# Reordering the opening of a fused attention, Fourier-mix and MLP kernel: sine tables before the exps, casts moved to VectorE, first weights triggered sooner

## The chip, the cores and the metric

The kernel runs on one core of one Trainium2 chip. The metric is the device time of one execution in microseconds (us). Before the change it is 305.07 us, the median of three runs (304.42 to 305.32); the profiled execution has a span of 303.2 us.

Five engines work side by side [...]: TensorE (PE, matrix products), VectorE (DVE), ScalarE (ACT), GpSimd (POOL) and SyncE (SP, which issues most DMAs). Each engine executes its own instructions strictly in the order of the program.

## The reference

For each of 8 batches, 8 heads, 512 rows and 32 state rows with head width 64, two attentions without projections are computed and laid one below the other; then a Fourier mix over both axes and a two-layer MLP follow.

```python
scores = scale * x @ state^T;   xread = softmax(scores) @ state       # 512 rows a head
scores2 = scale * state @ x^T;  sread = softmax(scores2) @ x          # 32 rows a head
x = concat([xread, sread])      # reshaped to (8, 544, 512): heads beside one another
u = x + real(fft(fft(x, axis=1), axis=2))
un = (u - mean(u)) / sqrt(var(u) + 1e-6)
out = u + relu(un @ w_ch1) @ w_ch2        # 512 -> 2048 -> 512
```

The Fourier mix is done as matrix products with tables of cosines and sines, which the kernel makes itself at its start. `w_ch1` and `w_ch2` are 4 MB of float32 each; they are cast to bfloat16 on their way into the core's memory, which only GpSimd's DMA queue does here.

## The kernel before

The program goes through the batches as a pipeline: while the two layers of the MLP of batch b run, attention and transform of the next batches are woven in between. What the change touches is the opening, some 20 us in which batch 0 goes through attention and transform with nothing to overlap with.

The order of the instructions is fixed by hand. The loads of x: a batch is seven DMAs of 256-byte rows, 1 MB in all. Those of batch 0 are issued first; those of batch 1 follow on the SP queue.

```python
    def load_x(b):
        ...
        parts = [(v[:, 0], xb[1:129]), (v[:, 1], xb[144:272]), (v[:, 2], xb[273:401]), (v[32:128, 3], xb[416:512]),
                 (v[0:15, 3], xb[129:144]), (v[16:31, 3], xb[401:416]), (row, xb[0:273:272])]
        ...                                  # batch 0: spread over the SP and ACT queues
        for o, rows in parts:
            nc.sync.dma_start(out=o, in_=rows)

    def cast_x(b, copy=nc.gpsimd.tensor_copy, lo=0, hi=4):     # float32 xs -> bfloat16 xin, by tiles of 128 rows
        copy(xin_bufs[b % 2][:, lo:hi, 1:513], xs_of[b].rearrange("p (i c) -> p i c", i=4)[:, lo:hi])
```

ScalarE begins with a table load for the exp and casts tiles 2 and 0 of x:

```python
    nc.scalar.activation(gate2[:, 1:2], gate2[:, 0:1], AF.Exp)
    state_ones(0, 2)
    state_blocks(0, 1)
    cast_x(0, nc.scalar.copy, 2, 3)
    cast_x(0, nc.scalar.copy, 0, 1)
```

GpSimd's part: it clears pads, makes the integers of the second table, clears XB and ZB, casts tiles 3 and 1, sets constants, and then triggers the first three of the four blocks of `w_ch1`:

```python
    load_x(1)
    ...
    for lo, k0, c, t in (...):
        nc.gpsimd.tensor_scalar(gi[:, lo:lo + 128], ...)       # four of these
    nc.gpsimd.memset(XB..., 0.0)
    nc.gpsimd.memset(ZB..., 0.0)
    for i in (3, 1):
        cast_x(0, lo=i, hi=i + 1)
    constants()
    clears(0)
    def first_weights(lo, hi):
        for q in range(lo, hi):
            nc.gpsimd.dma_start(out=w1[:, :, q * 512:(q + 1) * 512], in_=w1v[:, :, q * 512:(q + 1) * 512])
    first_weights(0, 3)
```

The opening itself (read and score are batch 0's attention by tiles; low_of, terms_of and out_of its first transform; warm(n) is n small matmuls with no use but to keep TensorE busy):

```python
    warm(11); turn_state(); second_table(); warm(5)
    copy = turn_x0(2); copy(); turn_products(); warm(3)
    exp2 = score(2); exp2()
    copy = turn_x0(0); copy(); warm(2)
    copy3 = turn_x0(3); turn_ends(); copy3(); read(2); warm(3)
    exp0 = score(0); copy1 = turn_x0(1); exp3 = score(3)
    exp0(); exp3(); copy1(); warm(2); read(0)
    exp1 = score(1); exp1(); read(3)
    ...                                   # XB and ZB filled by VectorE and GpSimd
    first_weights(3, 4)
    second_weights()                      # four blocks of w_ch2
    warm(6); read(1)
    sin_table(); sine_c(); sine_s()       # table load, cosines TC, sines TS
    warm(4); sread(); begin(); warm(6); low_of(0, 1); state_rows()
    ...                                   # low_of, even, odd, terms_of; minus(NC, TC), minus(NS, TS) on VectorE
    nc.gpsimd.tensor_copy(gate, XO0s[:, 0, 0:4])
    for i in range(4):
        cast_x(1, lo=i, hi=i + 1)         # batch 1 of x, GpSimd
    state_blocks(1, 2, nc.gpsimd.tensor_copy)
    ...                                   # the last terms_of and out_of
    s1, r1 = attend(1)
    exp_again()
    over_d(0); add_sums(0, 1); centre_sums(0, 1); over_d(1)
    turns1()                              # TensorE: 16 transposes of batch 1's x, all four tiles
    ...
    load_x(2)
    turned[2, 0](); turn_u(0, 1); ...; warm(4)
    L[0]()                                # first step of the MLP of batch 0
```

Of the kernel before, what the change touches and what calls it, by code (L numbers as in the profile page):

```python
# [30 lines left out]
def kernel(  # L31
# [17 lines left out]
    NM = 288  # L49
# [30 lines left out]
    for hh in range(4):  # L80
# [3 lines left out]
    nc.gpsimd.iota(ltq[:, :, 64:128], pattern=[[-1, 2], [-2, 64]], base=271, channel_multiplier=0)  # L84
    nc.gpsimd.iota(ltq[:, :, 128:144].rearrange("p q (a i) -> p q a i", a=2), pattern=[[1, 2], [272, 2], [2, 8]],
                   base=129, channel_multiplier=0)
    nc.gpsimd.iota(li[:, 0:128], pattern=[[2, 128]], base=1, channel_multiplier=0)
    nc.gpsimd.iota(li[:, 128:256], pattern=[[2, 128]], base=2, channel_multiplier=0)
    make_identity(nc, ident)
    mirror = singles.tile([128, 128], BF16, name="mirror")  # L90
    halves = ((halfpi, PI / 2), (pi_pos, PI * (1.0 - 1e-6)), (epst, eps), (mhalf, -0.5))
    sg = singles.tile([128, 1], F32, name="sg")
# [2 lines left out]
    def constants():  # L95
        for t, v in halves:
            nc.gpsimd.memset(t, v)
# [49 lines left out]
    def cast_x(b, copy=nc.gpsimd.tensor_copy, lo=0, hi=4):  # L147
        copy(xin_bufs[b % 2][:, lo:hi, 1:513], xs_of[b].rearrange("p (i c) -> p i c", i=4)[:, lo:hi])  # L148
# [27 lines left out]
    gate = singles.tile([128, 4], F32, name="gate")  # L176
    gate2 = singles.tile([128, 4], F32, name="gate2")
    nc.vector.memset(gate2, 0.0)
    nc.scalar.activation(gate2[:, 1:2], gate2[:, 0:1], AF.Exp)
    state_ones(0, 2)  # L180
    state_blocks(0, 1)
    cast_x(0, nc.scalar.copy, 2, 3)
    cast_x(0, nc.scalar.copy, 0, 1)


    w1 = singles.tile([128, DC, dff], BF16, name="w1")
# [40 lines left out]
    def turn(W, N, lf, cols, scratch):  # L227
        n = len(cols)
        f2d, q2d = scratch[:, 0:n * W], scratch[:, n * W:2 * n * W]
        f, q = [t.rearrange("p (n w) -> p n w", w=W) for t in (f2d, q2d)]  # L230
        def ends():
            absolute(q2d, f2d)

        def products():
            for i, c in enumerate(cols):
                nc.vector.scalar_tensor_tensor(f[:, i, :], in0=lf, scalar=pf[:, c:c + 1], in1=q[:, i, :], op0=ALU.mult, op1=ALU.add)

        for i, c in enumerate(cols):
            nc.vector.tensor_scalar(q[:, i, :], in0=lf, scalar1=pn[:, c:c + 1], scalar2=float(1 << 23), op0=ALU.mult, op1=ALU.add)
        nc.vector.tensor_scalar(q2d, in0=q2d, scalar1=float(1 << 23), scalar2=-float(N), op0=ALU.subtract, op1=ALU.mult)  # L240
        return f, q, products, ends

    shrink = 1.0 - 1e-6
    nc.vector.memset(lt[:, 279:280], 0)
    nc.vector.memset(lt[:, 287:288], 272)
    nc.vector.tensor_copy(pf, pi_)
    lo_, up_ = pf[:, 2:3], pf[:, 1:2]
    nc.vector.tensor_scalar(up_, in0=lo_, scalar1=145.0, scalar2=None, op0=ALU.is_ge)
    nc.vector.scalar_tensor_tensor(lo_, in0=up_, scalar=-16.0, in1=lo_, op0=ALU.mult, op1=ALU.add)
    nc.vector.scalar_tensor_tensor(lo_, in0=lo_, scalar=144.0, in1=lo_, op0=ALU.is_lt, op1=ALU.mult)  # L250
    nc.vector.scalar_tensor_tensor(lo_, in0=up_, scalar=272.0, in1=lo_, op0=ALU.mult, op1=ALU.add)
    pn = singles.tile([128, 3], F32, name="pn")
    nc.vector.tensor_scalar(pn, in0=pf[:, 0:3], scalar1=1.0 / Stot, scalar2=None, op0=ALU.mult)
    f1, q1, turn_products, turn_ends = turn(NM, Stot, lt, [0, 2], gen1)
# [5 lines left out]
    def second_table():  # L260
        nc.vector.tensor_scalar(gi, in0=gi, scalar1=dm - 1, scalar2=None, op0=ALU.bitwise_and)
# [12 lines left out]
    def sin_table():  # L274
        nc.scalar.activation(gate2[:, 2:3], gate2[:, 0:1], AF.Sin)
# [12 lines left out]
    def clear_pads(i):  # L288
        nc.gpsimd.memset(XFs[i][:, :, 512:514], 0.0)
        nc.gpsimd.memset(XRs[i][:, :, 0:514:513], 0.0)  # L290

    def clears(i):
        if i == 0:
            nc.gpsimd.memset(XO[:, :, 0:257:256], 0.0)
            nc.gpsimd.memset(XOl[:, 0:257:256], 0.0)
        nc.gpsimd.memset(XNs[i].rearrange("p a b -> p (a b)"), 0.0)
        nc.gpsimd.memset(XQls[i].rearrange("p a b -> p (a b)").bitcast(F32), 0.0)

    nc.gpsimd.memset(xs_of[1][0:1, 0:1], 0.0)  # L301
    clear_pads(0)
    clear_pads(1)
    load_state(1, 2)
# [6 lines left out]
    nc.gpsimd.memset(XB.rearrange("p a c -> p (a c)").bitcast(F32), 0.0)  # L311
    nc.gpsimd.memset(ZB.rearrange("p n c -> p (n c)").bitcast(F32), 0.0)
    for i in (3, 1):
        cast_x(0, lo=i, hi=i + 1)
    constants()
    clears(0)
    def first_weights(lo, hi):
        for q in range(lo, hi):
            nc.gpsimd.dma_start(out=w1[:, :, q * 512:(q + 1) * 512], in_=w1v[:, :, q * 512:(q + 1) * 512])
# [250 lines left out]
    def open_batch():  # L570
# [15 lines left out]
            nc.vector.tensor_copy(sT, p[:, 0:512].rearrange("p (a b) -> p a b", b=128))  # L586

        def turn(si):
            p = ps0.tile([128, 1024], BF16, name="xTp", tag="t", bufs=2)
            for pr in range(4):  # L590
                nc.tensor.transpose(p[:, pr * 128:(pr + 1) * 128], xin[:, si, 1 + 128 * pr:129 + 128 * pr], ident)
            return lambda: (nc.vector.tensor_copy if si else nc.scalar.copy)(
                xT[:, :, 128 * si:128 * si + 128], p[:, 0:512].rearrange("p (a b) -> p a b", b=128))

        def score(si):
            p = es[si] = ps0.tile([128, 512], F32, name="esp", tag="t" if si == 1 else "e", bufs=2)
            lo = 128 * si
            pieces = {1: [(0, slice(lo + 127, lo - 1, -1))],
                      3: [(0, slice(lo, lo + 32)), (32, slice(lo + 127, lo + 31, -1))]}.get(si, [(0, slice(lo, lo + 128))])
            for g in range(2):  # L600
                for o, rows in pieces:
                    n = abs(rows.stop - rows.start)
                    for hp in range(2):
                        nc.tensor.matmul(p[:, 128 * g + o:128 * g + o + n], lhsT=sT[:, 2 * g + hp, :],
                                         rhs=xT[:, 2 * g + hp, rows], start=(hp == 0), stop=(hp == 1))
            for pr in range(4):
                hp, o = pr % 2, 256 + 64 * pr
                nc.tensor.matmul(p[:, o:o + 64].rearrange("p (h j) -> p h j", j=Ns), lhsT=xT[:, pr, lo:lo + 128],
                                 rhs=sT[:, pr, 64 * hp:64 * hp + 64].rearrange("p (h j) -> p h j", j=Ns)[:, :, ::-1],
                                 start=True, stop=True)  # L610
            return lambda: nc.scalar.activation(EE[:, si, :], p, AF.Exp, scale=scale)
# [80 lines left out]
    def transform(b):  # L692
# [9 lines left out]

        acc = {}

        def begin():
            for j, tag in enumerate("ttee"):
                acc[j] = ps0.tile([128, 512], F32, name="gp", tag=tag, bufs=2)
            for j in range(4):
# [314 lines left out]
    exp2()  # L1023
    copy = turn_x0(0)
# [12 lines left out]
    copy1()  # L1037
    warm(2)
    read(0)
    exp1 = score(1)  # L1040
    exp1()
# [15 lines left out]
    begin()  # L1057
    warm(6)
    low_of(0, 1)
    state_rows()  # L1060
    low_of(1, 1), low_of(2, 1), low_of(3, 1)
    even(1)
    minus(NC, TC)
    terms_of(0, 1), terms_of(1, 1)
    odd(1)
    minus(NS, TS)
    second_sines()
    second_halves()
    sine_low()
    low_of(0, -1), low_of(1, -1)  # L1070
    terms_of(2, 1), terms_of(3, 1)
    even(0)
    low_of(2, -1), low_of(3, -1)
    terms_of(0, 0)
    out_of(0)
    terms_of(1, 0)
# [146 lines left out]
```

## Time and profile before

| stage, us from the start of the span | PE busy | DVE busy | ACT busy | POOL busy | DMA share of 16 engines |
|---|---|---|---|---|---|
| 0 to 6 | 2.54 | 4.15 | 3.18 | 4.96 | 0.83 |
| 6 to 12 | 5.04 | 5.12 | 2.56 | 4.51 | 1.05 |
| 12 to 18 | 6.00 | 5.43 | 5.28 | 4.40 | 1.19 |
| 18 to 24 | 5.44 | 3.42 | 4.98 | 5.49 | 1.24 |
| 24 to 28 | 4.00 | 3.79 | 3.32 | 0.11 | 1.21 |
| 28 to 34 | 5.24 | 5.05 | 3.58 | 5.45 | 1.22 |

Each row is one stretch of the span with the busy time of the engines in it. [...] TensorE is busy nearly throughout from 6 us on, but in the opening much of that is warm-up matmuls, so its busy time there says nothing about need. The DMA engines are loaded from 2 us to about 38 us: first x, then the weights.

### The profile page before, as it was taken

To read this page: it belongs to the slowest core of one execution; us is meant where nothing else is said; L and a number is where in the kernel's file an instruction comes from. 1 tells how busy PE (TensorE), PEld (TensorE's weight loads), DVE (VectorE), ACT (ScalarE), POOL (GpSimd) and SP (SyncE) were. 2 spreads that over 40 slices of the span, in tenths; PEclk is the share of its full clock that TensorE was granted. 3 is DMA by queue.
4 is the path that set the end of the run, shared out by engine and by line. 5 is a ranking of instruction groups with operands and counts; after the bars stand their busy time and mean duration, and the time that the engine had idled before them with its cause. 6 is when DMAs were issued, how large, how long until landed. Compare 5 with 4: busy or idle time off the path is not lost.

```text
span 303.2 us, 6030 instructions
## 1 busy us (share of the span) xinstructions
PE 288.2 (95%) x2310; PEld 165.6 (55%) x2341; DVE 182.1 (60%) x447; ACT 133.2 (44%) x248; POOL 92.9 (31%) x220
## 2 busy tenths in 40 slices
PE   4999897889999999999999999999999999999996
PEld 3889885444544545456544554445444544555443
DVE  7878895677879385755727575675668474000012
ACT  5687564436633553244533545244524442334300
POOL 6794564290371044301315022702240031000000
PEclk9999999999999999999999999999999999999999
DMA  8999954944934954459332695253333123600345
GB/s 156 191 204 198 203 99 98 214 90 104 175 88 71 205 131 82 105 93 220 95 81 55 146 183 90 68 121 77 82 91 69 37 69 87 138 3 35 71 132 145
DMA packets 110794, 34.86 MB, mean 115 GB/s; under 512 B 101950, under 2 KB 106302, under 8 KB 110766
## 3 DMA queue, kind: packets, MB, share of 16 engines
q1 hardware_dynamic: 100046, 28.72, 45.2%
q0 software_dynamic: 4224, 4.19, 8.3%
q10 hardware_dynamic: 6496, 1.57, 2.5%
q8 instruction: 18, 0.29, 0.4%
q14 instruction: 10, 0.08, 0.1%
HBM read 22.41 MB, written 14.02 MB: 120 GB/s over the span
## 4 chain that ended last, share of the span: by engine, by line
PE 76%; SPq 9%; DVE 5%; POOL 5%; DMA 2%; issue 2%; ACT 0%; POOLq 0%; DVEq 0%
PE po L978 34%; PE ph L914 32%; SPq L145 7%; PE gp L777 2%; SPq L387 1%; PE po L970 1%; DMA gen<-s_dram 1%; POOL stb L168 1%; DMA xs<-in_x_dram 1%; PE yp L674 1%; POOL w L324 1%; PE yp L673 1%; PE esp L431 1%; PE eTp L443 1%; PE xfp L456 1%
## 5 line engine op out<-in xcount | busy, mean ns | idle before, releaser
L978 PE MATMUL po<-w,hT 128*128 128x512 bf16 x481 | 122.2, 379 | 1.3 <-issue 0.6
L916 ACT ACTIVATE hT<-ph 128x512 bf16<-128x512 f32 x112 | 66.8, 597 | 121.2 <-PE ph L914 115.4
L914 PE MATMUL ph<-unT,w 128*128 128x512 bf16 x432 | 112.0, 379 | 0.7
L914 PEld LDWEIGHTS <-w 128*128 128x128 bf16 x576 | 50.6, 98 | 46.6 <-issue 0.5
L978 PEld LDWEIGHTS <-hT 128*128 128x128 bf16 x496 | 46.7, 98 | 46.6
L945 DVE SCALAR_TENSOR_TENSOR ot<-po,rstd,U 128x512 f32<-128x512 f32 (+2 forms) x33 | 24.1, 731 | 51.2 <-PE po L978 49.0
L781 POOL COPY GL<-G 128x128 bf16<-128x128 bf16 x7 | 2.0, 291 | 73.1 <-ACT G L778 73.1
L678 DVE TENSOR_TENSOR U<-yp,XR 128x512 f32<-128x512 f32 x14 | 9.5, 681 | 24.6 <-PE yp L674 24.6
L342 POOL TENSOR_TENSOR rstd<-mv,epst 128x1 f32<-128x1 f32 x34 | 8.1, 238 | 45.6 <-DVE mv L338 45.6
L336 DVE BATCH_NORM_STATS2 st<-U 128x6 f32<-128x512 f32 x32 | 21.8, 682 | 0.0
L343 POOL TENSOR_TENSOR rstd<-rstd,mhalf 128x1 f32<-128x1 f32 x34 | 20.4, 601 | 2.7
L924 PE MATMUL ph<-unT,w 128*128 128x128 bf16 x256 | 15.8, 219 | 0.3 <-DVE unT L846 0.3
L778 ACT CAST G<-gp 128x288 bf16<-128x288 f32 x28 | 13.1, 481 | 6.6 <-PE gp L777 6.5
L924 PEld LDWEIGHTS <-w 128*128 128x128 bf16 x256 | 14.8, 98 | 0.6 <-issue 0.4
L148 POOL CAST xin<-xs 128x512 bf16<-128x512 f32 (+1 forms) x11 | 13.3, 1233 | 1.6 <-DMA xs<-in_x_dram 1.6
L836 DVE TENSOR_SCALAR ub<-U,mv 128x512 bf16<-128x512 f32 x24 | 12.2, 508 | 1.1 <-DVE mv L338 0.3
L926 ACT ACTIVATE hT<-ph 128x512 bf16<-128x512 f32 x16 | 9.5, 596 | 6.3 <-PE ph L924 6.3
L513 POOL COPY XT<-XR 32x514 bf16<-32x514 bf16 x6 | 3.6, 603 | 22.7 <-DVE XR L465 22.6
L465 DVE TENSOR_TENSOR XR<-xrp,rs 128x512 bf16<-128x512 f32 x14 | 9.7, 694 | 0.5
L465 DVE TENSOR_TENSOR XF<-xfp,rs 128x512 bf16<-128x512 f32 x14 | 9.7, 692 | 0.5
L1010 PE MATMUL warm<-ident 128*128 128x128 bf16 x54 | 6.2, 261 | 3.5 <-POOL xs L301 3.5
L678 DVE TENSOR_TENSOR U<-yp,XF 128x510 f32<-128x510 f32 x14 | 9.5, 676 | 0.0
(240 smaller groups left out, 376.3 us busy)
## 6 DMA issues: line engine op xcount, KB each, us to landing
xs<-in_x_dram SPq DMA_DIRECT2D x22, 256.0 KB, 4.2
w<-in_moe_w_ch_dram POOLq DMA_DIRECT2D x8, 512.0 KB, 11.6
out_dram<-ot SPq DMA_DIRECT2D x15, 256.0 KB, 3.5
r_dram<-ot SPq DMA_DIRECT2D x14, 256.0 KB, 2.3
out_dram<-r_dram SPq DMA_DIRECT2D x14, 256.0 KB, 3.6
xs<-in_x_dram SPq DMA_DIRECT2D x8, 192.0 KB, 4.6
xs<-in_x_dram ACTq DMA_DIRECT2D x2, 256.0 KB, 5.6
l_dram<-ot SPq DMA_DIRECT2D x2, 256.0 KB, 2.0
```

The lines of the kernel that those rows point to most:

```text
L145: nc.sync.dma_start(out=o, in_=rows)
L148: copy(xin_bufs[b % 2][:, lo:hi, 1:513], xs_of[b].rearrange("p (i c) -> p i c", i=4)[:, lo:hi])
L336: nc.vector.bn_stats(st6, u)
L343: nc.gpsimd.tensor_tensor(rstd, rstd, mhalf, op=ALU.pow)
L465: nc.vector.tensor_tensor(ov, in0=p[ps, :, 0:256].rearrange("p g (h d) -> p g h d", d=D), in1=rs[ps].unsqueeze(3).to_broadcast([n, 2, 4, D ...
L678: nc.vector.tensor_add(u.rearrange("p (k r) -> p k r", r=2), p.rearrange("p (r k) -> p k r", r=2)[:, 0:u.shape[1] // 2, :], x.rearrange("p ...
L778: nc.scalar.copy(G[:, j, :].rearrange("p (i q) -> p q i", q=2), p[:, 0:NM].rearrange("p (q i) -> p q i", q=2))
L914: nc.tensor.matmul(ph[:, o:o + n], lhsT=w1[:, c, f * 128:(f + 1) * 128], rhs=un_of[key][:, c, :], start=(c == 0), stop=(c == DC - 1))
L916: nc.scalar.activation(hT[:, per * i:per * i + per, :].rearrange("p a b -> p (a b)"), ph, AF.Relu, scale=-1.0 / 512 if key == 0 else -1.0 ...
L924: nc.tensor.matmul(ph[:, o:o + 128], lhsT=w1[:, c, f * 128:(f + 1) * 128], rhs=un_of[key][:, c, 128 * r:128 * r + 128], start=(c == 0), st ...
L945: nc.vector.scalar_tensor_tensor(ot[:, cols], in0=po_of[i][:, 0:cols.stop - cols.start], scalar=rstd, in1=u[:, cols], op0=ALU.mult, op1=AL ...
L978: nc.tensor.matmul(po_of[i], lhsT=h_of[key][:, f, i * 128:(i + 1) * 128], rhs=w2[:, f, :], start=(f == 0), stop=(f == FC - 1))
```

## The change

It reorders the opening. The stated aims are four: the angles and the sine and cosine tables are made ahead of all exps; the last tiles of x are cast by VectorE; the negated tables NC and NS are made by ScalarE; the first weights are triggered sooner. With this go the places of some warm-up matmuls, PSUM tags, the splitting of the angle computation into smaller steps, and the order of the terms of the first transform.

```diff
+    make_identity(nc, ident)
     nc.gpsimd.iota(li[:, 0:128], ...)
     nc.gpsimd.iota(li[:, 128:256], ...)
-    make_identity(nc, ident)
...
-    nc.scalar.activation(gate2[:, 1:2], gate2[:, 0:1], AF.Exp)
+    nc.scalar.activation(gate2[:, 1:2], gate2[:, 0:1], AF.Sin)
     cast_x(0, nc.scalar.copy, 2, 3)
-    cast_x(0, nc.scalar.copy, 0, 1)
...
     def minus(o, i):
-        nc.vector.tensor_scalar(o, in0=i, scalar1=-1.0, scalar2=None, op0=ALU.mult)
+        nc.scalar.mul(o, i, -1.0)
...                       (angles: the same steps, pn for the two columns apart, memsets of lt behind pf)
     nc.gpsimd.memset(xs_of[1][0:1, 0:1], 0.0)
+    constants()
     clear_pads(0)
...
                                 op0=ALU.mult, op1=ALU.add)
-    nc.gpsimd.memset(XB..., 0.0)
-    nc.gpsimd.memset(ZB..., 0.0)
-    for i in (3, 1):
-        cast_x(0, lo=i, hi=i + 1)
-    constants()
-    clears(0)
-    first_weights(0, 3)
+    first_weights(0, 2)
...
-            return lambda: (nc.vector.tensor_copy if si else nc.scalar.copy)(
+            return lambda: (nc.scalar.copy if si == 1 else nc.vector.tensor_copy)(
...
+    turn_products()
+    turn_ends()
+    sine_s()
+    sine_c()
+    exp_again()
     warm(11)
     turn_state()
-    second_table()
     warm(5)
     copy = turn_x0(2)
     copy()
-    turn_products()
+    second_table()
     warm(3)
     exp2 = score(2)
     exp2()
+    for i in (0, 3, 1):
+        cast_x(0, nc.vector.tensor_copy, i, i + 1)
+    nc.gpsimd.tensor_copy(gate, xin_bufs[0][:, 1, 1:5])
+    nc.gpsimd.memset(XB..., 0.0)
+    nc.gpsimd.memset(ZB..., 0.0)
+    clears(0)
+    first_weights(2, 4)
     copy = turn_x0(0)
     copy()
-    warm(2)
     copy3 = turn_x0(3)
-    turn_ends()
     copy3()
-    read(2)
-    warm(3)
-    exp0 = score(0)
     copy1 = turn_x0(1)
-    exp3 = score(3)
-    exp0()
-    exp3()
     copy1()
     warm(2)
+    exp0 = score(0)
+    exp0()
+    read(2)
+    exp3 = score(3)
+    exp3()
     read(0)
...
-    first_weights(3, 4)
     second_weights()
-    warm(6)
+    warm(4)
     read(1)
+    sread()
+    begin(0, 1, 2, 3)
+    minus(NC, TC)
+    minus(NS, TS)
     sin_table()
-    sine_c()
-    sine_s()
-    warm(4)
-    sread()
-    begin()
-    warm(6)
-    low_of(0, 1)
+    warm(2)
+    low_of(0, 1), low_of(1, 1)
     state_rows()
...                       (low_of with both signs, then terms_of; second_sines and sine_low earlier)
```

The line `gate` that is added makes GpSimd wait until VectorE has cast tile 1 of x before it clears XB and triggers the other two blocks of `w_ch1`. The loads of x and of the states, the casts of batch 1, and everything from batch 1 on stay as they were, at the same places in their engines' orders.

More of the change, by code (lines that the diff above doesn't have):

```diff
@@ L236, in products, with counts, rests @@
                 nc.vector.scalar_tensor_tensor(f[:, i, :], in0=lf, scalar=pf[:, c:c + 1], in1=q[:, i, :], op0=ALU.mult, op1=ALU.add)
-        for i, c in enumerate(cols):
+        def counts(i):
+            c = cols[i]
             nc.vector.tensor_scalar(q[:, i, :], in0=lf, scalar1=pn[:, c:c + 1], scalar2=float(1 << 23), op0=ALU.mult, op1=ALU.add)
-        nc.vector.tensor_scalar(q2d, in0=q2d, scalar1=float(1 << 23), scalar2=-float(N), op0=ALU.subtract, op1=ALU.mult)
-        return f, q, products, ends
+        def rests():
+            nc.vector.tensor_scalar(q2d, in0=q2d, scalar1=float(1 << 23), scalar2=-float(N), op0=ALU.subtract, op1=ALU.mult)
+        return f, q, products, ends, counts, rests
     shrink = 1.0 - 1e-6
+    pn = singles.tile([128, 3], F32, name="pn")
+    f1, q1, turn_products, turn_ends, turn_counts, turn_rests = turn(NM, Stot, lt, [0, 2], gen1)
+    lo_, up_ = pf[:, 2:3], pf[:, 1:2]
+    nc.vector.tensor_copy(pf, pi_)
+    nc.vector.tensor_scalar(up_, in0=lo_, scalar1=145.0, scalar2=None, op0=ALU.is_ge)
+    nc.vector.tensor_scalar(pn[:, 0:1], in0=pf[:, 0:1], scalar1=1.0 / Stot, scalar2=None, op0=ALU.mult)
+    nc.vector.scalar_tensor_tensor(lo_, in0=up_, scalar=-16.0, in1=lo_, op0=ALU.mult, op1=ALU.add)
     nc.vector.memset(lt[:, 279:280], 0)
     nc.vector.memset(lt[:, 287:288], 272)
[L246 to L249, printed above, removed]
     nc.vector.scalar_tensor_tensor(lo_, in0=lo_, scalar=144.0, in1=lo_, op0=ALU.is_lt, op1=ALU.mult)
+    turn_counts(0)
     nc.vector.scalar_tensor_tensor(lo_, in0=up_, scalar=272.0, in1=lo_, op0=ALU.mult, op1=ALU.add)
-    pn = singles.tile([128, 3], F32, name="pn")
-    nc.vector.tensor_scalar(pn, in0=pf[:, 0:3], scalar1=1.0 / Stot, scalar2=None, op0=ALU.mult)
-    f1, q1, turn_products, turn_ends = turn(NM, Stot, lt, [0, 2], gen1)
+    nc.vector.tensor_scalar(pn[:, 2:3], in0=pf[:, 2:3], scalar1=1.0 / Stot, scalar2=None, op0=ALU.mult)
+    turn_counts(1)
+    turn_rests()
     gi = gen2[:, 0:512].bitcast(I32)
@@ L297, in clears, with first_weights @@
         nc.gpsimd.memset(XQls[i].rearrange("p a b -> p (a b)").bitcast(F32), 0.0)
+    def first_weights(lo, hi):
+        for q in range(lo, hi):
+            nc.gpsimd.dma_start(out=w1[:, :, q * 512:(q + 1) * 512], in_=w1v[:, :, q * 512:(q + 1) * 512])
     nc.gpsimd.memset(xs_of[1][0:1, 0:1], 0.0)
+    constants()
     clear_pads(0)
@@ L310 @@
                                 op0=ALU.mult, op1=ALU.add)
-    nc.gpsimd.memset(XB.rearrange("p a c -> p (a c)").bitcast(F32), 0.0)
-    nc.gpsimd.memset(ZB.rearrange("p n c -> p (n c)").bitcast(F32), 0.0)
-    for i in (3, 1):
-        cast_x(0, lo=i, hi=i + 1)
-    constants()
-    clears(0)
-    def first_weights(lo, hi):
-        for q in range(lo, hi):
-            nc.gpsimd.dma_start(out=w1[:, :, q * 512:(q + 1) * 512], in_=w1v[:, :, q * 512:(q + 1) * 512])
-    first_weights(0, 3)
+    first_weights(0, 2)
     def second_weights():
@@ L588, in turn @@
         def turn(si):
-            p = ps0.tile([128, 1024], BF16, name="xTp", tag="t", bufs=2)
+            p = ps0.tile([128, 1024], BF16, name="xTp", tag="r" if si == 1 else "t", bufs=2)
             for pr in range(4):
                 nc.tensor.transpose(p[:, pr * 128:(pr + 1) * 128], xin[:, si, 1 + 128 * pr:129 + 128 * pr], ident)
-            return lambda: (nc.vector.tensor_copy if si else nc.scalar.copy)(
+            return lambda: (nc.scalar.copy if si == 1 else nc.vector.tensor_copy)(
                 xT[:, :, 128 * si:128 * si + 128], p[:, 0:512].rearrange("p (a b) -> p a b", b=128))
         def score(si):
-            p = es[si] = ps0.tile([128, 512], F32, name="esp", tag="t" if si == 1 else "e", bufs=2)
+            p = es[si] = ps0.tile([128, 512], F32, name="esp", tag="t" if si in (1, 3) else "e", bufs=2)
             lo = 128 * si
@@ L703, in transform, with begin @@
         acc = {}
[L705 to L708, printed above, removed]
+        def begin(*js):
+            for j in js:
+                acc[j] = ps0.tile([128, 512], F32, name="gp", tag="eett"[j], bufs=2)
+            for j in js:
                 nc.tensor.matmul(acc[j][:, 0:NM], lhsT=XN[:, 0, :], rhs=xin_bufs[0][:, 0, 0:NM], start=True, stop=False)
@@ L1023 @@
     exp2()
+    for i in (0, 3, 1):
+        cast_x(0, nc.vector.tensor_copy, i, i + 1)
+    nc.gpsimd.tensor_copy(gate, xin_bufs[0][:, 1, 1:5])
+    nc.gpsimd.memset(XB.rearrange("p a c -> p (a c)").bitcast(F32), 0.0)
+    nc.gpsimd.memset(ZB.rearrange("p n c -> p (n c)").bitcast(F32), 0.0)
+    clears(0)
+    first_weights(2, 4)
     copy = turn_x0(0)
     copy()
-    warm(2)
     copy3 = turn_x0(3)
-    turn_ends()
     copy3()
-    read(2)
-    warm(3)
-    exp0 = score(0)
     copy1 = turn_x0(1)
-    exp3 = score(3)
-    exp0()
-    exp3()
     copy1()
     warm(2)
+    exp0 = score(0)
[3 more added lines that the diff above has]
+    exp3()
     read(0)
@@ L1047 @@
     nc.gpsimd.memset(XB[0:32, 1, 257:258], 0.0)
-    first_weights(3, 4)
     second_weights()
-    warm(6)
+    warm(4)
     read(1)
+    sread()
+    begin(0, 1, 2, 3)
+    minus(NC, TC)
+    minus(NS, TS)
     sin_table()
-    sine_c()
-    sine_s()
-    warm(4)
-    sread()
-    begin()
-    warm(6)
-    low_of(0, 1)
+    warm(2)
+    low_of(0, 1), low_of(1, 1)
     state_rows()
-    low_of(1, 1), low_of(2, 1), low_of(3, 1)
+    low_of(2, 1), low_of(3, 1)
     even(1)
-    minus(NC, TC)
+    second_sines()
+    second_halves()
+    low_of(0, -1), low_of(1, -1), low_of(2, -1), low_of(3, -1)
+    sine_low()
     terms_of(0, 1), terms_of(1, 1)
     odd(1)
[L1066 to L1070, printed above, removed]
     terms_of(2, 1), terms_of(3, 1)
     even(0)
-    low_of(2, -1), low_of(3, -1)
     terms_of(0, 0)
```

## The prediction

> **What bounds the kernel now.** I read three things in this order: the chain of work that ended last, the busy times by stage, and the DMA queues by stage. The chain and the stages:
>
> ```profile
> PE 76%; SPq 9%; DVE 5%; POOL 5%; DMA 2%; issue 2%; ACT 0%; POOLq 0%; DVEq 0%
> ```
> ```profile
> 0.00:22.00 22.00, 17.31 (x225) 15.14 (x226) 16.80 (x66) 14.64 (x27) 17.75 (x62) 1.00 1.06 183
> 22.00:43.00 21.00, 19.78 (x373) 18.94 (x371) 17.85 (x48) 14.24 (x26) 10.88 (x26) 1.00 1.07 181
> 43.00:75.00 32.00, 27.88 (x232) 15.14 (x234) 22.57 (x60) 15.44 (x30) 15.32 (x32) 1.00 0.55 117
> 75.00:303.00 228.00, 223.19 (x1490) 116.41 (x1513) 124.91 (x275) 88.85 (x167) 48.94 (x102) 1.00 0.47 102
> ```
>
> The columns are window, length, busy us of PE, PE weight loads, DVE, ACT, POOL, granted clock, DMA share, GB/s. TensorE carries the chain, and from 22 us on it idles only 1.2 + 4.1 + 4.8 us. So a microsecond gained or lost when the opening hands over at about 22 us moves the end, less what waits between 43 and 75 us can absorb. The rest of the chain (SPq, DMA) lies before 75 us: it runs through the loads of x. Hence the third view, the DMA queues; q1 is the SP queue (x), q0 GpSimd's queue (weights). First 9 to 12 us, x of batch 1 alone; then 26 to 36 us, x of batch 2 beside the weights:
>
> ```profile
> q1 hardware_dynamic: 2824, 0.71, 122.8%
> ```
> ```profile
> q0 software_dynamic: 1566, 1.55, 91.5%
> q1 hardware_dynamic: 1565, 0.39, 30.0%
> ```
>
> The columns are packets, MB and share of 16 engines. Alone, x moves at 2824/3 = 941 packets per us. Beside weights each queue moves 157 per us, packet for packet: x falls to a sixth. The SP timeline shows the same in its issues, seven each for batch 1 (before the weights) and batch 2 (among them):
>
> ```profile
> 6.97 5.03 SPq L145 DMA_DIRECT2D xs<-in_x_dram  x7
> ...
> 21.64 18.07 SPq L145 DMA_DIRECT2D xs<-in_x_dram  x7
> ```
>
> [...] the 128x576 step of the angles took 1.31 us beside GpSimd's work. [...] 11 matmuls of 128 columns at the start are spaced about 107 ns, the 16 transposes at 21.9 us about 56 ns.
>
> **The change part by part: the opening itself.** The three lines of VectorE and ScalarE that matter before:
>
> ```profile
> 4.88 1.31 DVE L240 TENSOR_SCALAR gen<-gen 128x576 f32<-128x576 f32 x1
> ...
> 7.34 1.29 DVE L236 SCALAR_TENSOR_TENSOR gen<-gen,pf 128x288 f32<-128x288 int32 x2
> 8.67 0.95 DVE L224 TENSOR_SCALAR gen<-gen 128x576 int32<-128x576 int32 x1
> ```
> ```profile
> 8.32 0.60 ACT L611 ACTIVATE EE<-esp 128x512 bf16<-128x512 f32 x1 [0.78 <-PE esp L608]
> ```
>
> Angles: the chain on VectorE starts at 2.54 now, released by the later integers of GpSimd; reordered it can start near 2.05. The steps to the end of the 1.31 took 3.6 us; the split of pn adds some 0.2, so about 5.7 (estimate), less if GpSimd contends less. Then signs 0.3, products 0.9 to 1.3 and absolute values 0.4 to 0.95: angles done at about 7.3 instead of 9.6. The sines (0.67 and 0.76) then end near 8.3, the table load and the dummy exp (1.28 + 0.1) near 9.7. **The first exp starts at about 9.7 instead of 8.32.** In return the table load and two sines that now lie at 13.06 to 15.80 become two negations and a table load. VectorE gets three casts (about 0.4 each by the spacing of like 128x512 float32 to bfloat16 operations, 1.2 in all), GpSimd loses 1.6. Nineteen warm-ups (56 to 107 ns each, 1 to 2 us) go, but most of them fill waits.
>
> Following the new order from there (scores 0.6 to 0.8, exp 0.6, reciprocal and product 0.9 a tile on VectorE), exp0 starts near 11.3, exp3 near 12.2, exp1 near 13; read(3) leaves VectorE near 14.2, and GpSimd's XB is ready at about 15.2. Now it is ready at 15.17, and low_of begins at 15.28. From there TensorE works without a gap to 20.14, and the same terms take the same 4.8 us. ScalarE is a near tie: its sequence up to sine_low ended at 19.30 and should end near 19.5. **Sum for the opening: 0.0, give or take 0.6 us**; the shorter tail behind the exps pays for their later start.
>
> **The weights.** Now GpSimd triggers them at 10.06, and q0's first packets appear near 12.4:
>
> ```profile
> 10.06 2.45 POOL L319 DMA_DIRECT2D w<-in_moe_w_ch_dram  x3
> ...
> 19.01 2.27 POOL L148 CAST xin<-xs 128x512 bf16<-128x512 f32 x4
> ```
>
> That is 2.4 us from trigger to flow, just as x of batch 1 finishes (its packets run from 8.0 to 13). After the change two blocks come directly behind the four integer operations, which end near 5.3; so they flow from 7.7, a little before x of batch 1 starts at 8.0. Two blocks are 2/8 of q0's 4224 packets, 1056; at 158 per us they last to about 14.4. The other two blocks wait for VectorE's cast of tile 1 (about 9.7) and GpSimd's clears (1.6), are triggered near 11.4 and flow from 13.8: no gap. The second weights, triggered near 15.3, join before those end. So q0 is never empty until 7.7 + 4224/158 = 34.4.
>
> x of batch 1 is 512 rows of 8 pieces, 4096 packets. Some 200 pass before the weights are at full rate; the remaining 3900 at 157 per us take 24.8 us: **x of batch 1 has landed at about 33 us instead of 13.** Nothing moves in its consumers: GpSimd casts it (the 19.01 line, which has no wait now), and TensorE has its transposes ahead of the MLP of batch 0:
>
> ```profile
> 21.89 1.06 PE L403 MATMUL xTp<-ident,xin 128*128 128x128 bf16 x16
> ```
>
> They need all four tiles. Landing 33 to 34, cast 0.6: they start at about 34.5, and TensorE stands still for 12.6 us. [...] Loss at this point 14.3. What comes back: the waits from 50 to 57 us (0.5 for a transposed x of batch 2, 1.2 + 1.2 behind it). Batch 2's loads are issued later but meet an empty weight queue, 4096/941 = 4.4 us, so its data should be ready about 8 us later while TensorE is 14 later; some 3 us of waits vanish. **Net +11, minus what a gap between q0's blocks gives: each 0.1 us of empty q0 passes some 80 packets more of x, half a microsecond of its landing.** I take off 1: about +10, 315.
>
> **The rivals.**
>
> *Rival 1, nothing starves.* If the weights flow later than 2.4 us after the trigger, or leave gaps, x of batch 1 mostly gets through. For it: x has slack from 13 to 19, some 6 us, and the added gate shows that someone thought of contention with x. Against it: the gate guards batch 0 only, and the trigger time follows from GpSimd's order. Then the sum of the opening rules: 303.5 to 306.
>
> *Rival 2, the whole gains.* The weights' queue ends 3 us earlier (34.4 for about 37.6), x of batch 2 lands sooner, the waits at 50 to 57 shrink, and the opening gains 0.5: 301 to 304. For it: the hole in the DMA traffic at 7.5 to 8.0 is filled. Against it: as in the main line, since total traffic is the same and only its order changes.
>
> *Rival 3, later exps alone cost.* ScalarE becomes the bound of the opening, with a fourth table load: 306 to 308. The chain before has ACT at 0%, which speaks for room.
>
> **Range and chances.** I give the starvation three quarters, with 308 to 320 and its middle near 315; a gap in q0 or a partly hidden wait is what makes it smaller. The rivals share the rest, nearly all within 2%. An eighth of the starvation falls under 311.2, where 2% ends. So 315.0, range 304.3 to 319.5; faster 0.03, same 0.27, slower 0.70.
>
> **What would show it.** Right: q0's first packets near 7.7; q1 near 157 per us from 8.5 on and x of batch 1 landing at 28 to 34; POOL's four casts waiting on DMA; a PE wait of 7 to 13 us on the 16 transposes; first exp at 9.3 to 10.2; low_of near 15.3. Wrong: casts at 18 to 19 without a wait, or q1 at 900 packets per us beside q0, or GpSimd's trigger well after 5.3. The opening's sum would be wrong if low_of began before 14.7 or after 16.

## The result, and the profile after

The change makes the kernel slower: **321.49 us**, the median of four runs (321.30 to 321.81), against 305.19 (304.42 to 305.57). The ratio is 1.0538, with a 95% interval of 1.0515 to 1.0561. That is 16.3 us more; the profiled execution has a span of 320.0 us instead of 303.2. The prediction was 315.0, with a range up to 319.5: it had the direction and the place, but not the size.

The chain of waits and the busy time by stage of the changed kernel; the columns are those of before (window, length, busy us of PE, weight loads, DVE, ACT, POOL, granted clock, DMA share, GB/s; a DMA share over 1 needs no second queue, since x alone had 122.8% before):

```profile
PE 81%; SPq 6%; DMA 5%; DVE 5%; issue 1%; ACT 0%; POOL 0%; ACTq 0%; POOLq 0%; DVEq 0%
```
```profile
0.00:22.00 22.00, 15.59 (x209) 12.42 (x209) 16.55 (x70) 17.27 (x31) 14.48 (x55) 1.00 1.06 175
22.00:43.00 21.00, 5.10 (x59) 4.68 (x59) 2.26 (x7) 2.10 (x3) 6.28 (x18) 0.59 0.99 168
43.00:75.00 32.00, 27.47 (x412) 22.52 (x414) 24.80 (x71) 18.48 (x34) 14.35 (x33) 1.00 0.39 84
75.00:303.00 228.00, 225.69 (x1539) 117.79 (x1566) 132.78 (x297) 97.02 (x184) 56.02 (x115) 1.00 0.45 100
```

Nearly the whole loss lies in the second row. TensorE is busy for 5.10 us of 21 there, where it was busy for 19.78, and its granted clock is 0.59. VectorE and ScalarE do next to nothing either. Only the DMA engines are full, with a share of 0.99. The chain says which DMA: its DMA share went from 2% to 5%, and 12.08 us of that are one piece, the landing of x of batch 1 from 24.74 to 36.82.

The DMA queues of the changed kernel from 13 to 34 us (queue, packets, MB, share of 16 engines), and its seven loads of x of batch 1 on the SP timeline (start, duration, what):

```profile
q0 software_dynamic: 3284, 3.26, 91.5%
q1 hardware_dynamic: 3280, 0.82, 29.9%
```
```profile
6.74 19.50 SPq L145 DMA_DIRECT2D xs<-in_x_dram  x7
```

q0, the weights, and q1, x of batch 1, pass equal numbers of packets for 21 us, 156 per us each, where x alone had 941; such equal counts are called turns below. Issuing its seven loads now takes SP 19.50 us instead of 5.03, while its queue drains at a sixth of its pace. What follows is on the timelines of GpSimd and of TensorE; the brackets hold the idle time before an instruction and what ended it:

```profile
3.81 2.22 POOL L321 TENSOR_SCALAR gen<-gen,pf 128x128 int32<-128x128 int32 x4
5.97 1.72 POOL L310 DMA_DIRECT2D w<-in_moe_w_ch_dram  x2
...
17.25 0.62 POOL L148 CAST xin<-xs 128x512 bf16<-128x512 f32 x1
23.46 0.61 POOL L148 CAST xin<-xs 128x512 bf16<-128x512 f32 x1 [5.59 <-DMA xs<-in_x_dram]
30.05 0.61 POOL L148 CAST xin<-xs 128x512 bf16<-128x512 f32 x1 [5.97 <-DMA xs<-in_x_dram]
37.39 0.61 POOL L148 CAST xin<-xs 128x512 bf16<-128x512 f32 x1 [6.74 <-DMA xs<-in_x_dram]
```
```profile
24.13 0.29 PE L405 MATMUL xTp<-ident,xin 128*128 128x128 bf16 x1 [3.69 <-POOL xin L148]
38.06 1.68 PE L405 MATMUL xTp<-ident,xin 128*128 128x128 bf16 x14 [13.64 <-POOL xin L148]
```

Before, the four casts ran without a wait from 19.01 and the 16 transposes began at 21.89. Now each cast waits for its own tile. TensorE has its turn at the transposes at 20.22, does two of the sixteen, and stands still for 3.69 and 13.64 us. The MLP of batch 0, much of which could run by then (in experiment 6 twelve steps of it run from 22.27 to 33.81), comes behind the transposes in TensorE's program.

### The profile page after: what moved, and what is told of

Its sections match the earlier page's. It is cut to its first block, busy times and chain, and to the rows that moved or that the text cites. A ratio compares the mean times of both kernels' runs of the same rounds, so it can differ in the third digit from the quotient of the medians.

```text
span 320.0 us, 6004 instructions
## 1 busy us (share of the span) xinstructions
PE 287.9 (90%) x2295; PEld 164.6 (51%) x2326; DVE 180.4 (56%) x449; ACT 134.9 (42%) x251; POOL 91.1 (28%) x219
## 4 chain that ended last, share of the span: by engine, by line
PE 81%; SPq 6%; DMA 5%; DVE 5%; issue 1%; ACT 0%; POOL 0%; ACTq 0%; POOLq 0%; DVEq 0%
PE po L980 34%; PE ph L916 32%; SPq L145 6%; DMA xs<-in_x_dram 5%; PE ph L926 3%; PE gp L779 2%; DVE st L338 1%; PE po L972 1%; PE yp L676 1%; PE xfp L458 1%; PE yp L675 1%; PE xrp L458 1%; PE eTp L445 1%; PE esp L433 1%; DVE U L680 1%
## 5 line engine op out<-in xcount | busy, mean ns | idle before, releaser
L405 PE MATMUL xTp<-ident,xin 128*128 128x128 bf16 x16 | 2.2, 305 | 17.3 <-POOL xin L148 17.3
L148 POOL CAST xin<-xs 128x2048 bf16<-128x2048 f32 (+1 forms) x9 | 11.9, 1321 | 18.4 <-DMA xs<-in_x_dram 18.3
L848 DVE COPY unT<-tp 128x512 bf16<-128x512 bf16 x8 | 3.3, 413 | 20.2 <-PE tp L847 20.2
L405 PEld LDWEIGHTS <-xin 128*128 128x128 bf16 x16 | 1.6, 141 | 17.8 <-POOL xin L148 17.7
```

## The experiments

All compare with the kernel before on the same chip, whose medians beside the three groups were 305.31, 304.79 and 305.28.

**1. The new opening with the weights late.** All four blocks of `w_ch1` are triggered where the changed kernel triggers its last two; nothing else differs from it.

```diff
-    first_weights(0, 2)
...
-    first_weights(2, 4)
+    first_weights(0, 4)
```

> The changed kernel with one thing undone: no block of w_ch1 is triggered ahead of the gate; all four are triggered behind the clears, near 10.1 us, where the kernel before had them. Theory A (x of batch 1 starves behind the weights, and nothing else costs): x of batch 1 lands near 13 us, GpSimd's casts wait on no DMA, TensorE's 16 transposes start near 20.2 us instead of 38, and the time is 303.4 (a gain of 1.67 us at the hand-over kept) to 305 (given back at waits for x of batch 2). Rival B (the later order of exps, four table loads and ScalarE's negations cost something later on): over 306. Rival C (a large part of the 16 us lies elsewhere, for instance in the order of the MLP): over 310.

Measured: 305.35 (304.40 to 307.21), ratio 1.0002 (0.9980 to 1.0025). The trigger comes at 10.03. GpSimd's timeline of this kernel shows the four casts in one piece, with nothing in brackets:

```profile
17.53 2.27 POOL L148 CAST xin<-xs 128x512 bf16<-128x512 f32 x4
```

So the two early triggers are the whole loss of 16 us, and the three other aims together are worth nothing that shows. Yet the opening hands over sooner in this profile: the first matmul of the last transform step (`yp`) starts at 19.75 instead of 21.02 (by estimate 0.5 to 0.8 of this is TensorE's clock, as the last section tells). By like instructions the kernel is 1.27 us ahead of the one before until 32 us, 0.66 ahead from 37 to 65, and 0.31 behind from 66 on. The first step is a copy on VectorE that here lies beside a clear by GpSimd (29.69 to 30.89); this kernel first, then before:

```profile
29.86 1.17 DVE L514 COPY XT<-XR 32x514 bf16<-32x514 bf16 x1
```
```profile
31.14 0.28 DVE L513 COPY XT<-XR 32x514 bf16<-32x514 bf16 x1
```

The second step is among TensorE's waits of this kernel between 15 and 75 us (what waited, for what, us in total, times, longest):

```profile
PE xrp L457 <- DVE XF L466: 1.5, 1, 1.5
PE esp L432 <- DMA xT<-xin: 1.2, 1, 1.2
```

Both waits were 0.5 before. `esp` is for the transposed x of batch 2, whose DMA is issued at 43.58 here and at 43.37 before; its extra 0.7 costs nothing, because the wait behind it, for ScalarE's `E`, is 0.5 here and was 1.2. It is `xrp` that takes 1.0. It waits for VectorE, which waits for a copy by GpSimd, and GpSimd for a load of states; GpSimd's casts of these states in this kernel and before:

```profile
60.37 2.98 POOL L168 CAST stb<-gen 32x640 bf16<-32x640 f32 x4 [4.60 <-DMA gen<-s_dram]
```
```profile
60.07 2.98 POOL L168 CAST stb<-gen 32x640 bf16<-32x640 f32 x4 [3.64 <-DMA gen<-s_dram]
```

SP issues that load behind the transposed x of batch 2 and the seven loads of batch 3, so it keeps its time when TensorE comes sooner.

**2. The old opening with two early weights.** The kernel before, with two blocks triggered behind the four integer operations, at 5.10.

```diff
+    for q in range(2):
+        nc.gpsimd.dma_start(out=w1[:, :, q * 512:(q + 1) * 512], in_=...)
     nc.gpsimd.memset(XB..., 0.0)
...
-    first_weights(0, 3)
+    first_weights(2, 3)
```

> The kernel before with one thing added: two blocks of w_ch1 are triggered directly behind the four integer operations, near 5.2 us; all else stays. Theory A: weights flow from 7.4 to 7.7 us, x of batch 1 gets some 155 packets per us until about 35, the 16 transposes start at 36 to 38 us, time 319 to 322. Rival B (it takes the new order as well): under 312.

Measured: 315.97 (314.90 to 319.20), ratio 1.0336 (1.0305 to 1.0367). The starvation comes without the new opening, but is smaller than I expected. The DMA queues of this kernel from 13 to 15 us say why:

```profile
q1 hardware_dynamic: 1106, 0.28, 69.0%
q0 software_dynamic: 200, 0.19, 55.7%
```

The first two blocks are through before the third, triggered at 9.59, flows in full, so q0 runs nearly empty for about a microsecond. In these 2 us x gets 1106 packets instead of 312, some 800 more, and from 17 to 19 us it gets 795, again some 480 more. Together that is 8 us of sharing at 156 per us, and x starts only a good 1 us later here. But the transposes begin at 34.95 against 38.06, no more than 3.1 us sooner: from 28 to 34 us x passes 507 packets beside 1049 of the weights, so it no longer has a turn for each of theirs, and the last tile still comes late. Whether some of the 16 DMA engines were done with x by then and others not isn't on record. This profiled execution took 319.20, so its trace accounts for less than half of the gap between the median of 315.97 and the 321.49 of the change.

**3. The first two blocks just behind the added gate**, which waits for VectorE's casts of batch 0.

```diff
-    first_weights(0, 2)
...
     nc.gpsimd.tensor_copy(gate, xin_bufs[0][:, 1, 1:5])
+    first_weights(0, 2)
```

> The changed kernel with its first two blocks triggered behind the gate but ahead of the clears, near 8.8 us, so that they flow from about 10.9. Theory A puts a number on it: alone, x of batch 1 has passed some 2540 of 4096 packets by then (counted in the trace of the kernel before); the other 1560 at 155 per us take 10 us, landing near 21 to 22; the transposes start near 22.5 instead of 20.2 and the time is 305 to 307. If the weights' time of trigger did not matter but only its being ahead of the clears, 318 or more; if it did not matter at all, the same as with the trigger behind the clears.

Measured: 306.74 (305.72 to 307.67), ratio 1.0047 (1.0027 to 1.0067). Trigger at 8.73, and three casts run without a wait. The fourth line of the four on GpSimd's timeline of this kernel, and TensorE's wait that it causes:

```profile
22.61 0.61 POOL L148 CAST xin<-xs 128x512 bf16<-128x512 f32 x1 [2.89 <-DMA xs<-in_x_dram]
```
```profile
PE xTp L404 <- POOL xin L148: 1.9, 1, 1.9
```

From 5.97 to 8.73 the trigger moves by 2.8 us, and TensorE's wait goes from 17.3 us to 1.9. It grows so steeply because x alone passes 941 packets per us, and beside weights 156: a microsecond that x loses alone costs six beside them.

**4. One block early, the rest behind the clears**, so that q0 has a gap.

```diff
-    first_weights(0, 2)
+    first_weights(0, 1)
...
-    first_weights(2, 4)
+    first_weights(1, 4)
```

> The changed kernel with one block instead of two triggered early; the other three behind the clears. Theory A: the block flows from 8.1 to 11.5 us, the others from 12.2; x of batch 1 gets 0.7 us at full rate in between, has passed about 1000 packets by 12.2, and the other 3100 at 155 per us take 20 us: landing near 32 to 33, transposes near 34, time 315 to 318. If only the first megabyte in the way counted (a queue that is served in turn, block by block), half of the loss: 311 to 313.

Measured: 315.30 in one run; transposes at 31.40 after a wait of 9.83. In the gap, from 11 to 13 us, q0 passes 51 packets and x 1904, more than I had allowed for. That is the same sharing as in 2 and 3, seen from the side of a gap.

**5. The weights of the second layer behind the casts of batch 1.** They are what keeps q0 full from about 20 us on.

```diff
-    second_weights()
...                       (behind the casts of batch 1, ahead of state_blocks)
+    second_weights()
```

> The changed kernel with the four blocks of w_ch2 triggered behind GpSimd's casts of batch 1 instead of ahead of them. Theory A (packet for packet, no matter which weight): w_ch1's 2112 packets flow from 8 to about 22; by then x of batch 1 has passed some 2100 of 4096, the rest goes at 941 per us, landing near 25, transposes near 26 instead of 38, TensorE stalls 5 to 6 us; time 308.5 to 311. If what counts is that two blocks are first in the way, 318 to 322.

Measured: 313.42 (312.82 to 314.28), ratio 1.0293 (1.0261 to 1.0326). x landed at 25.8, near what I expected, and the transposes began at 26.62, but the time is 2.4 us above my highest figure. TensorE also waited 2.3 us for the state blocks, which my edit had put behind four triggers on GpSimd, and its matmuls came at half rate until about 33.9, by estimate from their spacing: 32 of the MLP took 2.67 us from 32.36, and 1.95 from 23.93 in the kernel before. Half the stream of weights did about half the damage (a ratio of 1.0293 against 1.0538); how the rest of the loss divides between these two is not settled.

**6. Batch 1's attention behind twelve steps of the MLP of batch 0**, to see whether TensorE's order alone makes the wait cost.

```diff
-    turns1()
...                       (its copies, scores and reads follow it)
+    turns1()             (behind twelve steps of the MLP)
```

> The changed kernel with attention of batch 1 (its transposes, scores and reads) moved in the program behind the first twelve steps of batch 0's MLP, so that TensorE has work while x of batch 1 crawls in. Theory A (the loss is the in-order wait of TensorE, not the late data in itself): no wait on the transposes over 3 us, but batch 1's attention now has little beside it; time 311 to 317. Rival: if the late data itself moves the end (through GpSimd, the load of batch 2 and what follows), 320 to 322 as before.

Measured: 316.02 in one run. TensorE's wait for the cast shrinks from 17.3 us to 4.2, and the time falls by only 5.5. Batch 1's attention now runs with nothing beside it and brings waits of its own: 1.6 for `eTp` and 1.0 for `xfp` that the changed kernel doesn't have. It also runs on a slower clock: granted are 5 tenths of full speed in both slices of the page from 39.3 to 55.0 us, and 1.00 from 43 to 54 us in the changed kernel. So the order is what turns the late landing into standstill, but undoing it moves the loss more than it removes it.

**7. Two of batch 1's tiles on ScalarE's queue**, the weights as early as in the change.

```diff
+        held = parts[1:3] if b == 1 else []
         for o, rows in parts:
-            nc.sync.dma_start(out=o, in_=rows)
+            (nc.sync; the two held by nc.scalar, behind exp_again() of the opening)
```

> The changed kernel with two of the four tiles of batch 1 issued by ScalarE's queue instead of SyncE's, behind the table load near 8.5 us; the weights stay early. Theory A in its sharper form ([...] two queues get two turns): x of batch 1 gets some 270 packets per us instead of 155, lands near 25, transposes near 26; ScalarE loses about 1 us to the two issues; time 309 to 313. Rival (both hardware queues share one turn, or bytes are shared, not packets): 319 to 322.

Measured: 305.25 (303.99 to 308.84), ratio 1.0013 (0.9993 to 1.0033). I had expected 309 to 313. The profiled execution took 308.84, so the reading rests on its packets and issue times. The DMA queues of this kernel from 12 to 18 us; q10 is ScalarE's:

```profile
q0 software_dynamic: 824, 0.81, 79.6%
q1 hardware_dynamic: 812, 0.20, 25.8%
q10 hardware_dynamic: 808, 0.21, 15.5%
```

Three queues take equal turns, 135 to 137 packets per us each, so x has two turns of three and gets 270 per us. The edit did a second thing: SP's loads of batch 1 began at 5.78 instead of 6.74, and some 1400 packets of x passed between 8 and 10 us, where the change passes 94. Both should help, and this run doesn't separate them. In this execution TensorE still waits 4.3 us at the transposes; how long it waits in one of the median's time isn't on record.

**8. Late weights, and two tiles of batch 2 on ScalarE's queue**: can the opening's 1.3 us be kept if batch 2 lands sooner?

```diff
+        held = parts[1:3] if b == 2 else []
...
-    first_weights(0, 2)
...
-    first_weights(2, 4)
+    first_weights(0, 4)
```

> The version with all weights triggered near 10 us (the opening of the changed kernel without the starvation), and two of the four tiles of batch 2 issued by ScalarE's queue. There the hand-over gained some 1.3 us but waits for the transposed x of batch 2 gave it back. If two queues get two turns, batch 2 lands nearer to 37 than to 41.8, its transposes start at 41 to 42.5 instead of 43.6 and the time is 303.8 to 305.0. If the two issues hold ScalarE up near 22 us, or the end of w_ch2 is what pins the transposes, 305 to 307.

Measured: 304.50 (304.10 to 305.98), ratio 0.9992 (0.9977 to 1.0006). From 28 to 36 us the three queues pass 1094 packets each, to the packet. But the transposed x of batch 2 is issued at 44.39, no sooner than before, and TensorE waits 2.0 us for it (in an execution of 305.98). A second turn takes bytes from the weights, and the engines hardly move more in all: 207 GB/s here, 197 in experiment 1 in the same 8 us.

**9. Experiments 3 and 7 together**: weights behind the gate, two tiles of batch 1 on ScalarE's queue.

```diff
+        held = parts[1:3] if b == 1 else []
...
-    first_weights(0, 2)
...
     nc.gpsimd.tensor_copy(gate, xin_bufs[0][:, 1, 1:5])
+    first_weights(0, 2)
```

> A version meant to beat both: the changed kernel with its first two blocks triggered behind the gate (near 8.7 us, flowing from 10.9), and two tiles of batch 1's x on ScalarE's queue. By 11 us some 2700 of 4096 packets have passed; the rest at two turns (270 packets per us) lands near 16 to 17, so no wait on the 16 transposes; TensorE's hand-over is that of the new order (about 0.4 to 1.3 us sooner than before), and the weights end 1 us sooner, near 37. If the transposed x of batch 2 moves up with them, 303.5 to 304.5; if the loads of batch 2 pin it as they did with all weights at 10 us, 304.5 to 305.5.

Measured: **304.53** (303.83 to 305.27, 22 runs) against 305.28, ratio 0.9972 (0.9957 to 0.9986). No wait is left on the transposes. From 8 to 12 us x passes some 3500 of its 4096 packets and the weights 11, so here x is nearly through before there is anything to share. This is the version that beats both kernels, the one before by 0.8 us. Where the 0.8 comes from isn't shown: the profiled execution took 305.07, and its lead of 0.56 us is gone behind `xrp`, which waits 1.1 us as in experiment 1.

**10. The same with batch 2 on two queues as well.**

```diff
-        held = parts[1:3] if b == 1 else []
+        held = parts[1:3] if b in (1, 2) else []
```

> As the version with the first blocks behind the gate and two queues for batch 1, and two queues for batch 2 as well. Two queues for batch 2 did not make its tiles land sooner with all weights at 10 us, since the loads then end together with the weights; so the same time as with one queue for batch 2, within 0.3 us: 303.5 to 305.3.

Measured: 305.25 (304.48 to 307.00), ratio 0.9998 (0.9980 to 1.0016): nothing gained, as 8 would have it, and the 0.8 of experiment 9 is gone, where I had expected to keep it.

**11. The kernel before with GpSimd's clears of XB and ZB behind its casts**, to measure what they cost VectorE's angles.

```diff
-    nc.gpsimd.memset(XB..., 0.0)
-    nc.gpsimd.memset(ZB..., 0.0)
     for i in (3, 1):
         cast_x(0, lo=i, hi=i + 1)
     constants()
+    nc.gpsimd.memset(XB..., 0.0)
+    nc.gpsimd.memset(ZB..., 0.0)
```

> The kernel before with one thing moved: GpSimd's clears of XB and ZB (they ran from 5.1 to 5.9 us, beside VectorE's 128x576 step of the angles) behind its two casts. If GpSimd's clears are what slowed that step, it takes 0.5 to 0.7 us instead of 1.31, and the chain of angles ends 0.6 sooner; if the step is slow by itself in the old order, it stays at 1.2 to 1.4. Time: within 1 us of the kernel before, since waits on the loads of batch 2 take back what the opening gains.

Measured: 305.28 in one run. The step that took 1.31 us before, on VectorE's timeline of this kernel:

```profile
4.87 0.59 DVE L240 TENSOR_SCALAR gen<-gen 128x576 f32<-128x576 f32 x1
```

The hand-over comes at 19.50 instead of 21.02, from the old order of the opening with two lines moved, though part of this too may be an earlier full clock: VectorE's first two reciprocals of batch 0, the second of which waits for TensorE, start 1.51 us apart here and 2.18 before. Again the time doesn't follow: TensorE waits 1.4 us at `esp` and 1.6 at `xrp`.

## Why the prediction was right in kind and short in size

**The main line held.** Triggers behind the integers, turn by turn with x, four casts that wait, a standing TensorE, a slow restart (a granted clock of 0.50 from 38 to 40 us, 1.00 from 41 on): each is in the trace, and experiment 1 shows that without the early triggers nothing of the loss is left. Rivals 1 and 2 fall with the result, and so does rival 3, since experiment 1 keeps the new exps at 305.35.

**The failed steps are terms of the sum.** The prediction went 12.6 (standstill) + 1.7 (a slow clock behind it, the author's estimate, which the trace before didn't show) − 3 (comes back) − 1 (a gap) = about +10. Measured as shifts of like instructions between the two profiles:

| term | predicted | measured | from |
|---|---|---|---|
| transposes begin later | 12.6 | 16.2 | 38.06 against 21.89 |
| slow clock | 1.7 | 1.0 | first MLP matmul 41.11 against 23.93 |
| VectorE's `ub` slowed | – | 0.9 | next step 43.81 against 25.71 |
| comes back | −3 | −1.3 | shift 18.1 there, 16.8 at the end |
| gap in q0 | −1 | in the first row, about −1 | 307 packets of x from 11 to 12 us, beside 146 |
| **sum** | **10.3** | **16.8** | spans 320.0 and 303.2 |

*"x of batch 1 has landed at about 33 us"*: it landed at 36.8 (the chain's DMA, 24.74 to 36.82). The prediction's own formula, with three inputs mended, gives most of this. I let x start at about 8.2, but its first packet beside the weights comes at 9.3: +1.1. I let "some 200 pass before the weights are at full rate"; none did (from 8 to 9 us q0 passes 89, q1 none): 200/156 = +1.3. The rate was 156, not 157: +0.2. That makes 9.3 + 4096/156 = 35.6; a gap, told of below, takes off 1.0, and the landing trails this by 2.2. Behind x on the same queue lie 256 packets of states; whether they cause the trail isn't shown. That the trigger came at 5.97 instead of 5.3, since the four integer operations took 2.22 us instead of 1.6, is a small part: q0 flowed from 8.0, not 7.7.

*"some 3 us of waits vanish"*: only 1.3 did, and elsewhere. The kernel stays 18.1 us behind until the place of the wait `xrp`, where 0.7 comes back, and 0.6 more comes back some 6 us later. The 0.5 for a transposed x went, but the wait behind it, for `E`, grew from 1.2 to 1.6. I took the two waits of 1.2 from 50 to 57 us to hang on the same late data, so that they would go too. They are for ScalarE: in the changed kernel one of them is 1.6 us and the other is still 1.2 us, with batch 2 long landed. TensorE's waits of the changed kernel from 15 to 90 us:

```profile
PE xTp L405 <- POOL xin L148: 17.3, 2, 13.6
PE tp L847 <- ACT E L438: 1.6, 1, 1.6
PE tp L847 <- ACT ub L836: 1.2, 2, 0.6
```

The name of the releaser in the profile before said this already: what waits for ScalarE's own chain isn't cured by a later start.

*"minus what a gap gives"*: the mechanism was real, as experiments 2 and 4 show by 1106 and 1904 packets. The working had excluded a gap between the first two blocks and the next, and there was none: 152 and 153 packets of the weights from 12 to 14 us, in two steps of 1 us. But one came between the first block and the second, as the queues of the changed kernel from 11 to 12 us show:

```profile
q1 hardware_dynamic: 307, 0.08, 45.0%
q0 software_dynamic: 146, 0.13, 78.9%
```

That passes some 155 packets more of x, or 1.0 us of its landing. So the 1 us that I took off was right in size by luck; it is contained in the 16.2.

*A term I didn't have*: behind the standstill GpSimd clears a 128x1320 buffer (42.27 to 43.47) just as VectorE makes `ub`; that this clear slows it is read from the overlap, and tested only at another step, in experiment 11. VectorE's timeline of the changed kernel; the same step took 0.49 us before:

```profile
42.09 1.66 DVE L817 TENSOR_SCALAR ub<-U,S 128x512 bf16<-128x512 f32 x1
```

**The opening** was given as 0.0, give or take 0.6. Its inner times came out sooner than predicted, on VectorE and on ScalarE of the changed kernel:

```profile
4.04 0.51 DVE L242 TENSOR_SCALAR gen<-gen 128x576 f32<-128x576 f32 x1
...
4.71 0.99 DVE L235 SCALAR_TENSOR_TENSOR gen<-gen,pf 128x288 f32<-128x288 int32 x2
5.74 0.60 DVE L223 TENSOR_SCALAR gen<-gen 128x576 int32<-128x576 int32 x1
```
```profile
8.63 0.58 ACT L613 ACTIVATE EE<-esp 128x512 bf16<-128x512 f32 x1
```

The angles are done at 6.3 (predicted 7.3), the first exp starts at 8.63 (predicted 9.3 to 10.2), and low_of at 13.37 (predicted near 15.3; under 14.7 was to count as wrong). So this step was wrong in its parts: I priced the new order with durations that GpSimd's clears had stretched. Experiment 11 shows it, with 0.59 for 1.31. Part of the sooner low_of is, by estimate, TensorE's clock, which the last section tells of. Where the second exp of the new order starts at 9.58 (the change and experiments 1, 5, 6 and 7), the hand-over lies at 19.35 to 19.75; the old order with later clears has 19.47 and 19.50 (experiments 2 and 11). Where that exp starts near 10.1 (experiments 3, 4 and 8; in 9, where that exp isn't on record, VectorE's first reciprocal starts at 10.45, against 10.40 in 3 and 4 and 9.71 in 1), the hand-over lies at 20.2 to 20.5, and in the kernel before, at full rate only from 11.37, at 21.02. So at a like clock the new order gains by this estimate some 0.5 to 0.8 us, no more than moving the clears does. In the time the sum held, by luck: 305.35 against 305.31. The reason is another than the one I gave. It isn't that gains and losses cancel before the hand-over: that came sooner, and the copy and the wait `xrp` shown in experiment 1 took it back. That `xrp` hangs on the order of SP's loads behind batch 2 is a reading of the times; experiment 8 tried to bring batch 2 sooner and couldn't.

## What to carry to other kernels

Before a transfer is triggered sooner, ask what it shares its engines with and who needs that first: at equal counts of packets, a load of 256-byte rows fell here from 941 packets per us to 156 beside packets of some 990 bytes (3.26 MB in 3284), and 2.8 us of trigger time were worth 15 us of standing TensorE. The load that had to come through beside the stream did better nearly finished before it (some 3500 of 4096 packets and 304.53 us in experiment 9) than left to share (321.49); a second queue gave it a second turn here (270 packets per us), but what that alone is worth isn't separated from an earlier start. And a gain at a hand-over is one only up to the next transfer that has its own clock: look for it in the waits that grow behind, as in experiment 1, where a lead of 1.27 us ended as 0.31 behind.

## What the hardware showed that I had not expected

- Turns were equal to about 0.1% over long stretches: 3284 and 3280 packets for two queues in 21 us, 1094 three times for three in 8 us (but 507 beside 1049 near the end of x in experiment 2). The second queue of x gave a second turn and hardly more bandwidth (197 GB/s with two queues, 207 with three).
- x on SP's queue started late where the weights already flowed. In the change SP's first load of batch 1 is issued at 6.74 and passes its first packet at 9.3; in the kernel before, the issue is at 6.97 and packets come from 8.0. In experiment 2 the issue is at 6.68 and one packet has passed by 10.5. Why isn't settled.
- VectorE's operations took longer beside GpSimd's clears: 1.31 against 0.59 us for 128x576, which experiment 11 tested; 1.66 against 0.49 for `ub` and 1.17 against 0.28 for the copy of experiment 1, which are read from the overlap. None of this is a wait for a semaphore: the operations themselves are longer.
- TensorE's matmuls of 128 columns come at full rate, some 56 ns apart where they were 107 apart, from 7.05 us in the change and from 11.37 in the kernel before. Runs with the same TensorE program as the change differ in this too: from 7.0 to 11.3 us TensorE gets through 65 matmuls in 3.79 busy us in experiment 1 (65 in 3.72 in the change), but through 50 in 4.25 in experiment 4; the last exp of batch 0, which waits for TensorE, starts at 11.07 in experiment 1 and at 12.24 in experiment 3. What sets the moment isn't shown. By estimate it moves the hand-over of the new order by some 0.8 us (19.35 to 19.75 against 20.2 to 20.5), so single profiles of an opening can't be compared without it.
